# Four small moves in an attention and mixture-of-experts kernel: two in the opening, two where the experts take over

## The chip, the cores and the metric

The kernel runs on one NeuronCore of one Trainium2 chip. The core has five engines with a queue each: PE (matrix products), ACT (ScalarE), DVE (VectorE), POOL (GpSimd) and SP (SyncE, which here issues the DMAs). An engine works its queue off in order and waits on semaphores for the others. The metric is the device time of one execution in microseconds (us), the median of several runs. Times inside an execution are counted from the first instruction.

## The reference

Three stages in a row, all in float32:

```python
# 1 attention, 4 batches x 8 heads x 576 positions x 64
scores = scale * q @ k.T ; cum = cumsum(max(s, 0))
scores = where(causal, -1e9, scores + min(-(cum_i - cum_j), 0))
x = softmax(scores) @ v                      # -> 2304 tokens x 512
# 2 mixture of 8 experts, each token goes to its best one
xn, en = x / |x|, emb / |emb|
p = softmax(xn @ en.T / tau) ; e = argmax(p)
x = p[e] * (relu(x @ w1[e]) @ w2[e])         # 512 -> 1024 -> 512
# 3 gated layer
out = ((x @ wa) * (x @ wb)) @ wo             # 512 -> 1536 -> 512
```

## The kernel before

**Attention (0 to about 258 us).** Work goes by units, a unit being two heads of one batch; there are 16. For a unit, PE transposes k and q, ACT and DVE split them into a high and a low part (tiles `KH` and `sp`, `KS` and `ql`), and SP copies the queries' high part into `QS` (line 535). The scores then come from PE, DVE takes the row minimum (line 647), ACT the exponential (line 653), PE transposes the result and multiplies by v. What each engine does when is decided at build time by a small planner: the class `Sched` keeps a free time per engine and a heap of pending steps, each pushed with a ready time, an engine and a duration (`V.push(ready, engine, duration, fn)`). PE's items are taken from several lists, the first that is ready by these estimates. So a number in a push moves instructions in the engines' queues, and nothing moves at run time.

Two pushes matter here. `signs(1)` (line 1228) writes a sign pattern into eight rows of `ql`, the second of two buffers, for the second unit on. `norm` (line 1252) scales the embeddings of the experts by their norm and by tau: four DVE steps (lines 1245 to 1248) on tile `x`, which PE transposes later in `e_item`.

**Handover (258 to 300 us).** Tokens have been sorted to their experts: POOL scatters the rows into `xs` in DRAM. The experts are then taken in order of their size, not of their index. A value is loaded into all engines (line 1760), and a branch around a rarely used overflow part follows (line 1704): each engine jumps over it. Around it stand matmuls of no use, which only keep PE going (`idle`, counts in `WARM`). Then the first expert begins: `xload(0)` loads its rows `xg` from `xs` (line 1372, three DMAs), `xtr0` transposes them (line 1382) in two passes, 256 and 96 rows, four transposed slices `d` each, and ACT and DVE split them into `xh` and `xl`. `zfill(1)` writes zeros (`zrow`, line 1257) behind the second expert's rows in `xs`; since it writes the tensor that `xload(1)` reads, that load waits for it.

**Experts.** Weights come in eight blocks for each expert, of 512 KB: 0 to 3 from w1, 4 to 7 from w2. `wload2` issues the next block's DMA into tile `st` (line 243), `wsplit2` splits the oldest one that is loaded: ACT casts both halves (line 273), DVE or POOL subtract (line 281). Tiles `w0` to `w7` take the blocks of the first, third, ... expert, `v0` to `v7` those of the second, fourth, ... . Blocks 0 to 6 of the first expert are loaded and partly split in the attention stage.

In `products(e, f, prev)` PE does the first layer of slice f (line 1553, into `h`) and then the second layer of the slice before (line 1578, into `y`), which needs `hh` (ACT's relu, line 1561) and `hl` (DVE, line 1562) of that slice. Twelve matmuls make each. The loop behind it issues row loads, the next expert's transposes (`xtr`, line 1397, at slices 3 to 6) and one split and one load at a slice.

**Gated layer (about 490 us to the end).** The same with two first layers; it is not touched.

Of the kernel before, what the change touches and what calls it, by code (L numbers as in the profile page):

```python
# [34 lines left out]
PEND = (10, 1, 1)  # L35
WARM = (30, 84, 2, 0, 20, 10, 3)
LAT = 140.0
GATE = 3000.0
DRAIN = 93.0
LATP = 215.0  # L40
# [104 lines left out]
def moe_kernel(tc, q, k, v, s, emb, tau, w1, w2, wa, wb, wo, out, dbg=None):  # L145
# [36 lines left out]
    with left, right:  # L182
# [56 lines left out]

        def slot_load(src):  # L240
            t = slot([128, 1024], F32, "st")
            d = t if len(src.shape) == 2 else t.rearrange("p (a c) -> p a c", a=src.shape[1])
            nc.sync.dma_start(out=d, in_=src)
            return t
# [44 lines left out]
        if True:  # L289
# [32 lines left out]
            def ptnext():  # L322
                return pts[-TB]
# [503 lines left out]
            def e_item():  # L827
                def need():
                    return [ptnext()] if sdone[0] >= 8 else None

                def emit(end):
                    pt = ps_t.tile([128, 512], F32, name="pt")
                    for p in range(NP):
                        nc.tensor.transpose(
                            out=pt[:, E * p:E * p + E], in_=en[:, 128 * p:128 * p + 128], identity=ident[:E, :E]
                        )
                    rel = Tok()
                    pts.append(rel)

                    def f(_):  # L840
                        for h in range(2):
                            r = slice(64 * h, 64 * h + 64)
                            nc.vector.tensor_copy(
                                out=enbd[r, :, h, :], in_=pt[r, :E * NP].rearrange("p (a e) -> p a e", a=NP)
                            )

                    V.push(end, "D", 200, f, lambda t: setattr(rel, "t", t))

                return (need, 430.0, emit)
# [372 lines left out]
            def boot2():  # L1222

                blank(nc.gpsimd, kbs[1], S)
                blank(nc.gpsimd, qls[1], S - 64)
                for x in (qbs[1], z0s[1]):
                    nc.gpsimd.memset(x, 0.0)
                V.push(now[0] + 7000, "D", 840, lambda _: signs(1))
                nc.gpsimd.affine_select(
                    out=ltri, in_=ones, pattern=[[1, 128]], compare_op=ALU.is_gt, fill=0.0, base=0, channel_multiplier=-1  # L1230
                )
                nc.gpsimd.iota(iota8, pattern=[[1, E]], base=0, channel_multiplier=0, allow_small_or_imprecise_dtypes=True)
                for x in (oh, lg, sc[:, 0, :], rk, enbd, ixs):
                    nc.gpsimd.memset(x, 0.0)
                nc.gpsimd.memset(ss, 1.0)
                nc.gpsimd.memset(zrow, 0.0)
                nc.gpsimd.tensor_scalar(out=tie, in0=iota8, scalar1=-1.0, scalar2=float(E - 1), op0=ALU.mult, op1=ALU.add)
                nc.gpsimd.memset(tie[:, 0:1], FIRST + E - 1)
                for x, w in enumerate(CAPS):
                    nc.gpsimd.memset(caps[:, x:x + 1], float(w))  # L1240

            def norm():

# [7 lines left out]

                V.push(now[0] + 9000, "D", 900, f2)

# [87 lines left out]
            hp = pool(right, "hp", 2, side="right")  # L1341
            mxp = pool(right, "mxp", 4, side="right")
            keep = pool(right, "keep", 1, side="right")
# [33 lines left out]
            def xtr0():  # L1377
                t = xhs[0] = [xhp.tile([128, 4, GT], F32R, name=x)[:, :, :CAPS[0]] for x in ("xh", "xl")]
                for a0, a1 in ((0, 256), (256, CAPS[0])):
                    for d in range(4):  # L1380
                        for a in range(a0, a1, 128):
                            nc.tensor.transpose(
                                out=yb[d][:, a:a + 128], in_=xgs[0][:, a // 128, 128 * d:128 * d + 128], identity=ident
                            )
                        nc.scalar.copy(out=t[0][:, d, a0:a1], in_=yb[d][:, a0:a1])
                        nc.vector.tensor_tensor(
                            out=t[1][:, d, a0:a1], in0=yb[d][:, a0:a1], in1=t[0][:, d, a0:a1].bitcast(F32), op=ALU.subtract
                        )

            def xtr(e, d):  # L1390
# [31 lines left out]

            def wload2():
                if loaded[0] < len(jobs):
                    key = jobs[loaded[0]][0]
                    stg[key] = slot_load(slot_src(who(key[0]), key[1]))
                    loaded[0] += 1
# [329 lines left out]

            wload2()
            idle(WARM[2])
# [6 lines left out]
            count(0)  # L1766
            for j in range(4, 7):
                for x in range(2):
                    lo_op("DG"[j == 6], wstate[j], slots[0, j], 512 * x, 512 * x + 512)
            for _ in range(2):  # L1770
                misc.pop(0)()
            zfill(1)
            for _ in range(3):
                wload2()
            xtr0()
            prev = None
            for e in range(E):
                for f in range(8):
# [3 lines left out]
                    prev = (e, f)  # L1782
                    if (e, f) == (0, 1):
                        xload(1)
# [11 lines left out]
                    if e == E - 1 and f == 7:  # L1796
                        yload(1)
                    for _ in range(2 if (e, f) == (0, 1) else 1):
                        wsplit2()
                        wload2()  # L1800
# [81 lines left out]
```

## Time and profile before

| | |
|---|---|
| runs (3), median, lowest to highest | 956.17 us, 954.9 to 956.58 |
| profiled execution: time / span | 953.78 us / 952.1 us |
| PE busy | 917.8 us, 96% of the span |
| DVE, ACT, POOL busy | 516.9, 432.0, 256.4 us |
| granted TensorE clock, mean | 0.994 of full |
| PE's share of the chain that ended last | 68% |

The profile shows one execution. PE is close to full, so time is lost or gained only where PE waits; an idle engine elsewhere costs nothing by itself. "idle before <- releaser" in a row is the time an engine stood still ahead of an instruction, and the instruction that ended it. SPq is SP's queue: the time there is that of issuing a DMA, not of its transfer. [...]

### The profile page before, as it was taken

Reading aid. Unit: us, or ns where it says so; the run is one execution under the profiler, and the core shown is the slowest. Engines: PE = TensorE matmul, PEld = TensorE weight load, DVE = VectorE, ACT = ScalarE, POOL = GpSimd, SP = SyncE. Lnnn points to the kernel's source line nnn. Section 1 sums busy time; section 2 is a strip of 40 time slices with the busy share of each in tenths; the row PEclk is TensorE's granted clock in tenths of the full one; section 3 lists DMA queues with packets and bytes.
Section 4 is the critical chain, followed back from the end, with each engine's and each line's share of the span. In section 5 each row is a group of like instructions: output and inputs, shape, how many; then the busy total and the mean of one; then the engine's idle time right before and its main releaser. Section 6 shows DMA issues by size and latency. Waiting matters only on the chain.

```text
span 952.1 us, 17669 instructions
## 1 busy us (share of the span) xinstructions
PE 917.8 (96%) x6447; PEld 839.7 (88%) x6448; DVE 516.9 (54%) x1319; ACT 432.0 (45%) x1074; POOL 256.4 (27%) x308
## 2 busy tenths in 40 slices
PE   8998999999889999999999999999999999999996
PEld 7777878777669999999998999999999999999995
DVE  8788888798756343455678888732212222222112
ACT  6677888876645444455544434421211111121111
POOL 6122323256234333344303344632001001001001
PEclk9999999999999999999999999999999999999999
DMA  5774555526277667677736444412010010000000
GB/s 136 175 154 105 143 116 123 140 71 185 96 221 241 225 193 218 215 226 241 223 106 204 129 118 131 90 26 75 1 34 34 1 34 34 1 1 34 1 1 34
DMA packets 102259, 107.90 MB, mean 113 GB/s; under 512 B 58445, under 2 KB 72733, under 8 KB 102157
## 3 DMA queue, kind: packets, MB, share of 16 engines
q1 hardware_dynamic: 98573, 97.04, 36.0%
q0 software_dynamic: 3552, 9.46, 2.8%
q8 instruction: 65, 1.06, 0.5%
q14 instruction: 37, 0.30, 0.1%
q10 hardware_dynamic: 32, 0.04, 0.0%
HBM read 77.90 MB, written 20.44 MB: 103 GB/s over the span
## 4 chain that ended last, share of the span: by engine, by line
PE 68%; DMA 2%; DVE 0%; issue 0%; SPq 0%; POOLq 0%; ACT 0%; DVEq 0%; ACTq 0%
PE h L1643 16%; PE x L1643 16%; PE y L1664 14%; PE y L1578 10%; PE h L1553 10%; DMA xg<-xs 1%; PE x L1397 1%; PE x L1664 1%; PE h L1664 1%; DMA xs<-zrow 1%; DMA yt<-mx 0%; DVE xl L1631 0%; SPq L1372 0%; POOLq L1878 0%; DVE mx L1654 0%
## 5 line engine op out<-in xcount | busy, mean ns | idle before, releaser
L1654 DVE TENSOR_TENSOR mx<-x,mx 128x384 f32<-128x384 f32 x72 | 39.9, 555 | 225.1 <-PE x L1643 225.0
L1655 ACT CAST hh<-mx 128x384 fp32r<-128x384 f32 x71 | 36.4, 512 | 159.0 <-DVE mx L1654 159.0
L1649 ACT COPY mx<-h 128x384 f32<-128x384 f32 x72 | 34.5, 479 | 150.8 <-PE h L1643 149.8
L1683 POOL DMA_INDIRECT out_dram<-mx,pmt x18 | 17.6, 979 | 292.5 <-DVE mx L1682 223.2
L653 ACT ACTIVATE z<-z,mn 128x192 f32<-128x192 f32 (+3 forms) x128 | 78.2, 611 | 37.9 <-DVE mn L647 37.2
L1643 PE MATMUL h<-xh,w 128*128 128x384 f32 x288 | 79.8, 337 | 1.3 <-ACT mx L1649 1.3
L1643 PE MATMUL h<-xh,v 128*128 128x384 f32 x288 | 79.7, 337 | 0.0
L1643 PE MATMUL x<-xh,w 128*128 128x384 f32 x288 | 78.9, 334 | 0.0
L633 PE MATMUL st<-KS,QS 128*128 128x288 f32 (+3 forms) x160 | 58.7, 374 | 9.4 <-DVE mn L647 7.4
L756 PE MATMUL pt<-ident,z 128*128 128x128 f32 x448 | 63.5, 277 | 3.3 <-ACT pT L180 1.6
L281 POOL TENSOR_TENSOR w<-st,w 128x512 fp32r<-128x512 f32 (+1 forms) x43 | 47.1, 1101 | 68.1 <-ACT w L273 57.8
L647 DVE CUSTOM_DVE_ANT_0 z<-st,maskb 128x192 f32<-128x192 f32 (+3 forms) x128 | 58.7, 477 | 9.5 <-PE st L636 7.3
L1562 DVE SCALAR_TENSOR_TENSOR hl<-h,hh 128x288 fp32r<-128x288 f32 (+6 forms) x64 | 31.2, 487 | 58.8 <-ACT hh L1561 58.8
L1656 DVE TENSOR_TENSOR hl<-mx,hh 128x384 fp32r<-128x384 f32 x71 | 39.7, 559 | 41.1 <-ACT hh L1655 41.1
L800 PE MATMUL xa<-pT,vn 128*64 128x128 f32 x896 | 60.0, 278 | 1.9 <-ACT pT L180 1.6
L281 POOL TENSOR_TENSOR v<-st,v 128x512 fp32r<-128x512 f32 x32 | 43.2, 1353 | 62.5 <-ACT v L273 48.7
L1664 PE MATMUL y<-v,hh 128*128 128x512 f32 x192 | 59.8, 392 | 0.0
L756 PEld LDWEIGHTS pt<-ident,z 128*128 128x128 f32 x448 | 49.9, 141 | 11.0 <-ACT z L653 4.3
L1553 PE MATMUL h<-xh,v 128*128 128x256 f32 (+2 forms) x256 | 59.0, 304 | 0.0
L1578 PE MATMUL y<-hh,v 128*128 128x256 f32 (+2 forms) x256 | 58.0, 300 | 0.0
L1553 PE MATMUL h<-xh,w 128*128 128x288 f32 (+3 forms) x256 | 57.8, 302 | 0.0
L800 PEld LDWEIGHTS xa<-pT,vn 128*64 128x64 f32 x896 | 47.9, 137 | 11.0 <-issue 5.6
(308 smaller groups left out, 2520.0 us busy)
## 6 DMA issues: line engine op xcount, KB each, us to landing
st<-in_moe_w_dram SPq DMA_DIRECT2D x64, 512.0 KB
QS<-sp SPq DMA_DIRECT2D x62, 128.0 KB
st<-in_moe_w_a_dram SPq DMA_DIRECT2D x12, 512.0 KB
st<-in_moe_w_b_dram SPq DMA_DIRECT2D x12, 512.0 KB
st<-in_moe_w_out_dram SPq DMA_DIRECT2D x12, 512.0 KB
xg<-yt SPq DMA_DIRECT2D x6, 768.0 KB
xg<-xs SPq DMA_DIRECT2D x7, 512.0 KB
kn<-in_k_dram SPq DMA_DIRECT2D x24, 128.0 KB
```

Source lines behind the costliest of these rows:

```text
L281: e.tensor_tensor(out=o[:, 1, a:b], in0=t[:, a:b], in1=o[:, 0, a:b].bitcast(F32), op=ALU.subtract)
L633: nc.tensor.matmul(st[:m, :wp], lhsT=qs[:, h, s0 - 64:s0 - 64 + m], rhs=ks[:, h, c0:c0 + wp], start=True, stop=False)
L647: nc.vector.tensor_tensor_reduce(out=z[:m, h, c0:c0 + w], in0=st[:m, :w], in1=maskb[:m, S - kk + c0:S - kk + c0 + w], op0=ALU.add, op1=ALU ...
L653: nc.scalar.activation(out=z[:m, h, :kk], in_=z[:m, h, :kk], func=AF.Exp, scale=-1.0, bias=m1, accum_out=rsum[:m, tid(b, c), 2 * p + h:2 * ...
L756: nc.tensor.transpose(out=pt[:, 128 * x:128 * x + 128], in_=zs[i][:, h, a0:a0 + 128] if c else z0s[u % 2], identity=ident)
L800: nc.tensor.matmul(xa[64 * h:64 * h + 64, :m], lhsT=v_[:m, 2 * p + h, :], rhs=locs[i][bk, h], start=bk == 0, stop=bk == c,)
L1553: nc.tensor.matmul(ph[:, :n], lhsT=w[:, hl, 128 * f:128 * f + 128], rhs=mv[:, d, :n], start=k_ == 0, stop=k_ == 11,)
L1578: nc.tensor.matmul(ys[e][d][:, :n], lhsT=w[:, hl, c0 + 128 * d:c0 + 128 * d + 128], rhs=mv[:, :n], start=f == 0 and k_ == 0, stop=f == 7 a ...
L1643: nc.tensor.matmul(p, lhsT=w[:, hl, d, c0:c0 + 128], rhs=mv[:, d, :], start=d == 0 and k_ == 0, stop=d == 3 and k_ == 2,)
L1654: nc.vector.tensor_tensor(out=g, in0=pp[1], in1=g, op=ALU.mult)
L1656: nc.vector.tensor_tensor(out=gl, in0=g, in1=gh.bitcast(F32), op=ALU.subtract)
L1664: nc.tensor.matmul(ots[i][t], lhsT=st[:, 128 * t:128 * t + 128], rhs=w[:, hl, c0:c0 + 512], start=f == 0 and k_ == 0, stop=f == 11 and k_ ...
```

## The change

- The planner gets `signs(1)` as a step of ACT, not of DVE.
- The scaling of the embeddings is pushed 16,000 ns ahead, not 9,000 (`NORM`), and `e_item` waits for it in the plan.
- One warming matmul fewer ahead of the branch, one fewer behind it.
- The load of block 7 of the first expert, issued ahead of the branch so far, is issued behind `xtr0`, and waits on the first transposed slice of its second pass.
- The low parts of blocks 5 and 6 go to POOL (block 5 was DVE's), and three of the small steps for the gate weights come ahead of the transposes instead of two.
- `xload(1)` goes out one slice earlier, after two weight blocks were issued instead of five; the splits and loads of the first two slices are counted anew.
- A pool of 512-column tiles gets five buffers instead of four.

```diff
-WARM = (30, 84, 2, 0, 20, 10, 3)
+WARM = (30, 84, 1, 0, 20, 10, 2)
+NORM = 16000.0
...
-        def slot_load(src):
+        def slot_load(src, after=None):
             t = slot([128, 1024], F32, "st")
             d = t if len(src.shape) == 2 else t.rearrange("p (a c) -> p a c", a=src.shape[1])
-            nc.sync.dma_start(out=d, in_=src)
+            x = nc.sync.dma_start(out=d, in_=src)
+            if after:
+                tc.add_manual_dep(x.ins, after, DEP, reason="rows first")
...
-                    return [ptnext()] if sdone[0] >= 8 else None
+                    return [ptnext(), ntok] if sdone[0] >= 8 else None
...
-                V.push(now[0] + 7000, "D", 840, lambda _: signs(1))
+                V.push(now[0] + 7000, "A", 1200, lambda _: signs(1, nc.scalar.copy))
...
-                V.push(now[0] + 9000, "D", 900, f2)
+                V.push(now[0] + NORM, "D", 900, f2, lambda t: setattr(ntok, "t", t))
...
-            mxp = pool(right, "mxp", 4, side="right")
+            mxp = pool(right, "mxp", 5, side="right")
...
+                        if a0 and d == 0:
+                            first = x.ins.name
+                return first
...
-            wload2()
             idle(WARM[2])
...
-            for j in range(4, 7):
+            for x in range(2):
+                lo_op("D", wstate[4], slots[0, 4], 512 * x, 512 * x + 512)
+            for _ in range(3):
+                misc.pop(0)()
+            for j in (5, 6):
                 for x in range(2):
-                    lo_op("DG"[j == 6], wstate[j], slots[0, j], 512 * x, 512 * x + 512)
-            for _ in range(2):
-                misc.pop(0)()
+                    lo_op("G", wstate[j], slots[0, j], 512 * x, 512 * x + 512)
+            turned = xtr0()
+            wload2(turned)
             zfill(1)
-            for _ in range(3):
-                wload2()
-            xtr0()
+            wload2()
...
-                    if (e, f) == (0, 1):
+                    if (e, f) == (0, 0):
                         xload(1)
...
-                    for _ in range(2 if (e, f) == (0, 1) else 1):
-                        wsplit2()
+                    for x in range(2 if e == 0 and f < 2 else 1):
+                        if f or x == 0:
+                            wsplit2()
                         wload2()
```

SP's queue at the handover, behind the branch, before the change. `st_4885` is block 0 of the second expert, `st_4887`, `st_4889` and `st_4955` are its blocks 1 to 3; block 7 of the first expert has gone out ahead of the branch.

```order
L1372 DMA xg_4837<-xs_95 96x512
L1257 DMA xs_95<-zrow_270 736x1x256
L243 DMA st_4885<-in_moe_w1_dram 128x1024
L243 DMA st_4887<-in_moe_w1_dram 128x1024
L243 DMA st_4889<-in_moe_w1_dram 128x1024
L243 DMA st_4955<-in_moe_w1_dram 128x1024
L1374 DMA xg_5010<-xs_95 128x2x512
L1375 DMA xg_5010<-xs_95 112x512
```

The same place after the change. `st_4911` is block 7 of the first expert, `st_4914` block 0 of the second, `st_4953`, `st_4955` and `st_5015` its blocks 1 to 3.

```order
L1377 DMA xg_4834<-xs_95 96x512
L244 DMA st_4911<-in_moe_w2_dram 128x2x512
L1262 DMA xs_95<-zrow_270 736x1x256
L244 DMA st_4914<-in_moe_w1_dram 128x1024
L1379 DMA xg_4945<-xs_95 128x2x512
L1380 DMA xg_4945<-xs_95 112x512
L244 DMA st_4953<-in_moe_w1_dram 128x1024
L244 DMA st_4955<-in_moe_w1_dram 128x1024
L244 DMA st_5015<-in_moe_w1_dram 128x1024
```

Block 7 now stands between the first expert's rows and the zeros; the second expert's rows stand ahead of its block 1, not behind its block 3.

ACT's queue from the first slice on, before the change (`w7` is block 7 of the first expert, `v0` to `v3` are blocks 0 to 3 of the second, `hh` the relu of a slice).

```order
L1561 ACTIVATE hh_4946<-h0_4631 128x352
L273 CAST w7_4950<-st_4637 128x512 x2
L1561 ACTIVATE hh_5006<-h1_4632 128x352
L273 CAST v0_5013<-st_4885 128x512 x2
L273 CAST v1_5020<-st_4887 128x512 x2
L1561 ACTIVATE hh_5076<-h0_4631 128x352
L273 CAST v2_5080<-st_4889 128x512
L1488 ACTIVATE lt_4629<-lt_4629 128x160
L1561 ACTIVATE hh_5137<-h1_4632 128x352
```

And after it:

```order
L1569 ACTIVATE hh_4941<-h0_4631 128x352
L276 CAST w7_4948<-st_4911 128x512 x2
L1569 ACTIVATE hh_5006<-h1_4632 128x352
L276 CAST v0_5010<-st_4914 128x512 x2
L276 CAST v1_5017<-st_4953 128x512 x2
L1569 ACTIVATE hh_5073<-h0_4631 128x352
L276 CAST v2_5077<-st_4955 128x512
L1569 ACTIVATE hh_5137<-h1_4632 128x352
```

Casts and relus keep their order; only the exponential `lt` has left this stretch, and the casts read tiles whose loads have moved in SP's queue.

DVE's queue in the opening, before the change (`ql_191` is the second sign pattern's buffer, the four rows from line 1245 are the scaling).

```order
L1207 SCALAR_TENSOR_TENSOR xT_165<-xT_163,nb,xT_164 128x576
L1154 CAST ql_191<-pick 8x512 x2
L178 COPY pT<-pt 128x512
L395 TENSOR_TENSOR KS<-pt,KH 64x512 x2
L647 ISA z,mn<-st,maskb 128x448
L1245 TENSOR_SCALAR mn<-mn 8x1
L1246 RECIPROCAL mn<-mn 8x1
L1248 TENSOR_SCALAR x<-x,mn 8x512
L402 SCALAR_TENSOR_TENSOR ql_191<-pt,sp 64x512 x2
L395 TENSOR_TENSOR KS<-pt,KH 64x64 x2
```

And after it:

```order
L1210 SCALAR_TENSOR_TENSOR xT_165<-xT_163,nb,xT_164 128x576
L179 COPY pT<-pt 128x512
L398 TENSOR_TENSOR KS<-pt,KH 64x512 x2
L650 ISA z,mn<-st,maskb 128x448
L398 TENSOR_TENSOR KS<-pt,KH 64x64 x2
L405 SCALAR_TENSOR_TENSOR ql_191<-pt,sp 64x512 x2
L179 COPY xT_566<-xa 128x128
L1250 TENSOR_SCALAR mn<-mn 8x1
L1253 TENSOR_SCALAR x<-x,mn 8x512
L701 ISA zf_196,mn<-st,bt_529 128x64
```

The sign pattern has left DVE's queue, and the scaling stands about a dozen instructions later, ahead of the first short score pass `zf`.

## Rows read from the trace of the kernel before

**Rows 1.** PE's waits over the whole trace: engine, line, releaser: us in total, times, longest.

```profile
PE st L633 <- DVE mn L647: 7.4, 16, 1.0
PE h L174 <- PEq L1704: 2.8, 1, 2.8
PE x L1397 <- DMA xg<-xs: 1.6, 2, 1.2
```

**Rows 2.** Stretches: PE, PEld, DVE, ACT, POOL busy (instructions); PEclk; DMA; GB/s.

```profile
22.00:32.00 10.00, 8.21 (x78) 6.50 (x79) 7.72 (x29) 6.16 (x19) 0.73 (x1) 1.00 0.64 147
300.00:498.00 198.00, 198.00 (x1462) 197.82 (x1462) 97.31 (x177) 101.08 (x215) 64.35 (x49) 1.00 0.66 208
```

**Rows 3.** Timeline, PE at the handover: start, length, instruction, idle before it.

```profile
270.57 1.32 PE L1382 MATMUL y<-ident,xg 128*128 128x128 f32 x4 [0.31 <-DVE xl L1386]
278.10 0.30 PE L1578 MATMUL y<-hh,w 128*128 128x288 f32 x1
281.26 0.30 PE L1578 MATMUL y<-hh,w 128*128 128x288 f32 x1
284.27 0.41 PE L1397 MATMUL x<-ident,xg 128*128 128x128 f32 x2 [1.25 <-DMA xg<-xs]
```

**Rows 4.** Chain that ended last, 240 to 300 us: start, length, what.

```profile
266.21 3.38 DMA xg<-xs
269.80 6.20 DMA xs<-zrow
276.73 8.23 DMA xg<-xs
```

**Rows 5.** Timelines, SP's issues and POOL's first work at the handover.

```profile
244.03 0.37 SPq L243 DMA_DIRECT2D st<-in_moe_w_dram  x1
...
264.81 1.83 SPq L1372 DMA_DIRECT2D xg<-xs  x3
276.11 0.39 SPq L1374 DMA_DIRECT2D xg<-xs  x1
...
261.38 2.48 POOL L281 TENSOR_TENSOR w<-st,w 128x512 fp32r<-128x512 f32 x2 [1.75 <-POOLq L1704]
```

**Rows 6.** Timeline, ACT at the handover.

```profile
273.92 1.13 ACT L273 CAST w<-st 128x512 fp32r<-128x512 f32 x2
277.68 1.14 ACT L273 CAST v<-st 128x512 fp32r<-128x512 f32 x2 [2.07 <-DMA st<-in_moe_w_dram]
279.19 1.14 ACT L273 CAST v<-st 128x512 fp32r<-128x512 f32 x2 [0.37 <-DMA st<-in_moe_w_dram]
280.24 0.46 ACT L1561 ACTIVATE hh<-h 128x352 fp32r<-128x352 f32 x1
```

**Rows 7.** Stretches at the handover, columns as in rows 2.

```profile
261.50:264.50 3.00, 0.20 (x1) 0.00 (x0) 1.87 (x3) 1.43 (x2) 2.36 (x2) 1.00 0.05 14
264.70:268.00 3.30, 3.30 (x5) 1.22 (x5) 2.84 (x8) 0.00 (x0) 0.00 (x0) 0.50 0.55 149
283.00:284.30 1.30, 0.05 (x2) 0.06 (x1) 0.52 (x1) 0.71 (x3) 0.60 (x1) 1.00 1.05 269
...
271.10:275.00 3.90, 3.90 (x28) 3.58 (x28) 2.19 (x8) 2.22 (x7) 0.00 (x0) 1.00 0.91 186
275.00:280.60 5.60, 5.60 (x44) 5.60 (x44) 2.23 (x4) 3.07 (x8) 2.77 (x3) 1.00 1.02 377
```

**Rows 8.** Timelines of the opening: DVE, SP, PE.

```profile
18.30 1.25 DVE L1154 CAST ql<-pick 8x512 fp32r<-8x512 f32 x2
22.69 0.14 DVE L1245 TENSOR_SCALAR mn<-mn 8x1 f32<-8x1 f32 x1
23.11 0.53 DVE L1248 TENSOR_SCALAR x<-x,mn 8x512 f32<-8x512 f32 x1
...
27.18 2.48 SPq L535 DMA_DIRECT2D QS<-sp  x4
...
31.87 0.39 PE L633 MATMUL st<-KS,QS 128*128 128x256 f32 x1
```

More of the change, by code (lines that the diff above doesn't have):

```diff
@@ L1240, in boot2 @@
                     nc.gpsimd.memset(caps[:, x:x + 1], float(w))
+            ntok = Tok()
             def norm():
@@ L1381, in xtr0 @@
                         for a in range(a0, a1, 128):
-                            nc.tensor.transpose(
+                            x = nc.tensor.transpose(
                                 out=yb[d][:, a:a + 128], in_=xgs[0][:, a // 128, 128 * d:128 * d + 128], identity=ident
@@ L1421, in ringpool, with wload2 @@
                 return ringa0 if nm in ("w0", "w1", "w2", "w3") else rings[nm] if nm in rings else ringa1[0] if nm[0] == "w" else rings[nm[0]]
-            def wload2():
+            def wload2(after=None):
                 if loaded[0] < len(jobs):
                     key = jobs[loaded[0]][0]
-                    stg[key] = slot_load(slot_src(who(key[0]), key[1]))
+                    stg[key] = slot_load(slot_src(who(key[0]), key[1]), after)
                     loaded[0] += 1
```

## The prediction

> **What bounds the kernel now.** I read the list of PE's waits first: PE waits for little, and the three entries that this change touches are DVE's score passes in the attention stage (7.4 us in 16 waits), the one jump at the handover (2.8) and the rows of the second expert (1.6 in two waits) [rows 1]. Then the stretches: from 300 us on PE is busy in all of 198 us, so whatever PE loses or gains before that is kept to the end, one for one [rows 2]. So only two places matter: the opening, up to about 32 us, and the handover, 258 to 300 us. There I read PE's timeline, the chain that ended last, SP's queue and ACT's queue. In the first expert PE goes through without a gap until it reaches the transposes of rows(1), for which it waits 1.6 us in two pieces, the longer 1.25 [rows 1, 3]. The chain says why: fill(1) (zeros, 6.20 us) must have landed before rows(1) may start, and rows(1) took 8.23 us, since four weight blocks lay ahead of it in the same queue [rows 4].
>
> **The handover, step by step.** Names: (e,j) is weight block j of expert e in their order of work (the first is 0), rows(e) its token rows, fill(e) the zeros, relu(0,f) ACT's pass on slice f of the first expert.
>
> 1. Load (0,7) goes from 244.03, where the queue was empty long before anyone needed it (14 GB/s in the stretch before rows(0)), to behind the first of the four second-pass transposes: these start at 270.57 and take 1.32 us, so the first is done at 270.9 [rows 3, 5, 7]. Rows(0), issued from 264.81 to 266.64, had the queue to themselves already, so the move gives them nothing [rows 5].
> 2. SP serves in order, so fill(1) now follows (0,7): 270.9, 0.37 for the issue, 0.2 (an estimate) for SP's register steps, so 271.5 instead of 269.80 [rows 4, 5]. It needs its 6.20 us [rows 4], and its data stand behind those of (0,7), 524 KB at 377 GB/s, 1.4 us [rows 7]; (0,7) starts 0.6 us ahead, so I add 0.8. It lands at 278.5; before, at 276.0.
> 3. Rows(1) waits for that and goes out at 278.6. Rows(0) took 4.8 us from first issue (264.81) to landing (266.21 + 3.38 = 269.59) for 704 KB [rows 4, 5]; 736 KB take 5.0, so 283.6. Block (1,0) lies ahead of it and is out by then.
> 4. Load (1,1), so far ahead of rows(1), now stands behind it. Blocks in a row land 1.5 us apart (277.68 and 279.19, when ACT, which was waiting for them, could start) [rows 6], so (1,1) lands at 285.1 instead of 279.19.
> 5. What is queued behind this wait decides. ACT's order is relu(0,1), casts of (1,0), casts of (1,1), relu(0,2), as before. Relu(0,2) ran at 280.24, right after those casts, and PE wanted it at 281.26: one microsecond of slack [rows 3, 6]. Now: 285.1, 1.14 for the casts, 0.46 for relu(0,2), 0.3 (an estimate) until DVE's low part follows: PE goes on at 287.0, 5.7 us after 281.26. Rows(1) is there by then, so the old wait of 1.6 is gone [rows 1]. Net 5.7 - 1.6 = +4.1 us.
>
> Bounds of that term: the shortest time from issue to landing in that chain is 3.38 us [rows 4]; (1,1), issued at 279.4, then lands at 282.8 and the wait is 3.4, net +1.8. If fill(1) too needs only 4.8, as rows(0) did, another 1.4 goes: net +0.4. If nothing of (0,7) is hidden, 0.6 comes on top: +4.7. I take +4.1, by the rows of the very same transfers.
>
> The casts of (0,7) themselves: by the 3.38 us it lands at 274.3, ACT's casts of 1.13 us, which ran at 273.92 without a wait, end at 275.4 and relu(0,1) at 275.9 [rows 4, 6]. PE wants that at 278.10 [rows 3], so this wait is hidden; without that cover it would cost what it is late. [...]
>
> [...] One such stretch, 3.3 us at half rate, costs 1.7; I take +1.2, with 0 and 1.8 as ends. [...]
>
> Two fewer warming matmuls: one stood ahead of the jump, and it is the jump that PE waits for there [rows 1]; the third one after it ran while rows(0) were still on their way. Nothing on the path. [...] I take +0.2, 0 to 1.7.
>
> The other moves cost nothing: POOL takes four subtractions of (0,5) and (0,6) instead of two, 1.24 us each from 261.38, done at 266.4, first wanted at 281.26 [rows 3, 5]; were they late, PE would wait that long. The exponential goes into ACT's idle time ahead of the transposes.
>
> **The opening.** DVE loses the second sign pattern (1.25 us at 18.30) and the four scaling steps (22.69 to 23.64, 0.95) [rows 8], 2.2 us in all in a stretch in which PE waits for DVE; ACT gets 1.25 ahead of its pass on the next unit's queries, and the scaling lies in DVE's gaps some 5 us later. PE is idle 1.8 of the 10 us from 22 to 32 [rows 2], so 1.8 is the most. But PE's next unit, at 31.87, needs four copies which SP issues from 27.18 to 29.66 [rows 8], and SP's order there is the same and full. By the 3.38 us from issue to landing [rows 4] the last, issued at about 29.1, cannot be there much before 31.9. So PE only arrives earlier and waits. I take -0.3; ends -1.8 and, if ACT's 1.25 is in the way, +1.2.
>
> **Sum.** +4.1 + 1.2 + 0.2 - 0.3 = +5.2 us. The profiled execution took 953.78 us (span 952.1 and 1.7 around it), so 959.0 by it. The median of the runs, 956.17, is 2.4 above; the same sum on it gives 961.4, my forecast.
>
> **Rivals.**
> - The load is only half as late. The queue overlaps transfers better than step 2 to 4 have it, (1,1) lands at about 282, and the wait is 2.6. For: both shortest rows above. Against: landings 1.5 us apart in issue order [rows 6]. +0.4 to +1.8 for that term, no clock loss, -0.3: 956.3 to 957.7. That is within 0.2%.
> - Faster: (1,1) lands in time. The place is ACT's casts ahead of relu(0,2), the point is a landing by 279.4 (281.26 less 1.14, 0.46 and 0.3). Then rows(1) early is pure gain, -1.6 [rows 1], and with the opening's -0.3 to -1.8 the time is 952.8 to 954.3. For: the wait for rows(1) is real. Against: (1,1) is issued no sooner than 279.2, behind a landing of fill(1).
> - Worse: after the long wait the clock stays down for a second stretch and the later blocks, all behind, hold ACT again in the next slices: another 1.7 and 1 to 2 us, 964 to 965.
> - That the change doesn't do what it says: the order of SP's queue shows (0,7) behind rows(0) and rows(1) ahead of (1,1), so I give it no chance of its own.
>
> **How the numbers follow.** Forecast 0.66 (own range 959.3 to 963.5), half as late 0.14 (a little of it slower), faster 0.11 (a little of it within the bound below), worse 0.09. What a measurement can tell from no change is 0.2%, 1.9 us, so 954.3 to 958.1. Slower: 0.77. Same: 0.13. Faster: 0.10. The range, 955.8 to 963.6, leaves out the faster case and the worse one.
>
> **What would show it.** In the profile of the changed kernel: a wait of PE of 5 to 6 us at the first expert's second-layer products, about 281 us, released by ACT's hh or DVE's hl; ahead of it ACT idle for 3 us or more for a weight block, right before relu(0,2); no more wait for rows(1); fill(1) issued near 271.5 and rows(1) near 278.6; then a stretch at a granted 0.50. In the opening, DVE's waits shorter and PE's first product of the second unit still near 31.5. I am wrong if ACT's casts of the second block start by 280, or if PE has no wait over 2 us between 270 and 300.

## The result, and the profile after

The changed kernel took 961.17 us (median of 7 runs, 959.25 to 964.23), the kernel before 955.68 beside it (7 runs, 953.97 to 956.58): a ratio of 1.0061, 95% interval 1.0048 to 1.0074, or 5.5 us more between the medians. A second measurement on another chip gave 963.26 against 956.72, 1.0072 (1.0053 to 1.0091). The profiled execution took 960.33 us, its span 958.6, 6.5 more than before.

PE's waits answer to [rows 1] (total, times, longest):

```profile
PE st L636 <- DVE mn L650: 6.5, 15, 1.0
PE h L175 <- PEq L1712: 4.8, 1, 4.8
PE y L1586 <- ACT hh L1569: 4.5, 1, 4.5
```

The wait for the second expert's rows is gone from the list. In its place stands one of 4.5 us for `hh`, on the second-layer products of the first expert. PE's timeline shows where, and answers to [rows 3]:

```profile
270.39 0.98 PE L1387 MATMUL y<-ident,xg 128*128 128x128 f32 x7 [0.90 <-DMA xg<-xs]
271.70 1.47 PE L1387 MATMUL y<-ident,xg 128*128 128x128 f32 x4 [0.32 <-DVE xl L1391]
...
288.16 0.40 PE L1586 MATMUL y<-hh,w 128*128 128x288 f32 x1 [4.49 <-ACT hh L1569]
288.72 0.43 PE L1586 MATMUL y<-hl,w 128*128 128x288 f32 x1 [0.16 <-DVE hl L1570]
...
291.35 0.84 PE L1405 MATMUL x<-ident,xg 128*128 128x128 f32 x3
...
295.33 0.49 PE L1405 MATMUL x<-ident,xg 128*128 128x128 f32 x3
...
305.81 0.32 PE L1561 MATMUL h<-xh,v 128*128 128x352 f32 x1
```

PE's products stop at 283.67 (288.16 less the 4.49 of its wait); the transposes of rows(1), 291.35, wait for nothing; the last row is the second expert's first product. SP's queue, against [rows 5]:

```profile
264.74 3.02 SPq L1377 DMA_DIRECT2D xg<-xs  x3
272.07 0.40 SPq L244 DMA_DIRECT2D st<-in_moe_w_dram  x1
272.90 0.66 SPq L1262 DMA_DIRECT2D xs<-zrow  x1
273.77 0.46 SPq L244 DMA_DIRECT2D st<-in_moe_w_dram  x1
279.86 0.39 SPq L1379 DMA_DIRECT2D xg<-xs  x1
280.47 0.33 SPq L1380 DMA_DIRECT2D xg<-xs  x1
281.00 8.51 SPq L244 DMA_DIRECT2D st<-in_moe_w_dram  x6
```

And ACT's, against [rows 6]:

```profile
275.81 0.47 ACT L1569 ACTIVATE hh<-h 128x352 fp32r<-128x352 f32 x1 [2.37 <-PE h L1561]
276.18 1.13 ACT L276 CAST w<-st 128x512 fp32r<-128x512 f32 x2
277.40 0.47 ACT L1569 ACTIVATE hh<-h 128x352 fp32r<-128x352 f32 x1
281.31 1.14 ACT L276 CAST v<-st 128x512 fp32r<-128x512 f32 x2 [3.45 <-DMA st<-in_moe_w_dram]
286.61 1.14 ACT L276 CAST v<-st 128x512 fp32r<-128x512 f32 x2 [4.16 <-DMA st<-in_moe_w_dram]
287.65 0.46 ACT L1569 ACTIVATE hh<-h 128x352 fp32r<-128x352 f32 x1
```

After relu(0,1) at 277.40 ACT stands idle 3.45 us for block (1,0), casts it, stands idle 4.16 us for block (1,1), casts that, and only then does relu(0,2) at 287.65, whose input had been there since about 280.5 (the first-layer products of slice 2 end there). The chain that ended last says the same, against [rows 4]:

```profile
265.17 5.18 DMA xg<-xs
...
272.07 0.40 SPq L244
...
272.90 6.82 DMA xs<-zrow
...
281.00 5.59 DMA st<-in_moe_w_dram
...
287.75 0.37 ACT hh L1569
...
288.14 0.54 DVE hl L1570
...
288.72 2.83 PE y L1586 x11
```

It runs rows(0), issue of (0,7), fill(1) 6.82 us, the two issues of rows(1), block (1,1) 5.59 us, its cast, relu(0,2), low part, PE. The transfer of rows(1), 8.23 us of the old chain, has left it. Three stretches, columns as in [rows 2] (PEclk, the granted clock as a share of full, is the third number from the end):

```profile
22.00:32.00 10.00, 8.31 (x74) 7.00 (x73) 7.14 (x24) 5.05 (x16) 0.72 (x1) 0.83 0.61 142
272.00:274.00 2.00, 2.00 (x9) 1.68 (x9) 1.58 (x6) 0.97 (x5) 0.00 (x0) 0.50 0.37 91
...
288.20:292.20 4.00, 3.84 (x16) 3.61 (x17) 3.25 (x7) 1.50 (x3) 2.22 (x2) 0.59 0.95 341
```

The granted clock was 0.83 from 22 to 32 us (1.00 in [rows 2]), 0.50 in the first slice's products up to 274 (1.00 in [rows 7], 271.1 to 275), and 0.59 behind the stall.

| | before | after | difference |
|---|---|---|---|
| first matmul behind the search | 258.25 | 258.31 | +0.06 |
| rows(0) landed | 269.59 | 270.35 | +0.8 |
| first slice's `hh` | 273.56 | 275.81 | +2.25 |
| second expert's first product | 298.85 | 305.81 | +7.0 |
| end of the span | 952.1 | 958.6 | +6.5 |

All of the loss lies between 265 and 306 us. Of it 0.5 comes back later, net; among the differences there, a wait of 1.3 us of the kernel before (line 1643, for `mx`) is gone. Whether the fifth buffer did that was not tried.

### The profile page after: what moved, and what is told of

It is laid out like the page before. It is cut to its first block, busy times and chain, and to the rows that moved or that the text cites. A ratio compares the mean times of both kernels' runs of the same rounds, so it can differ in the third digit from the quotient of the medians.

```text
span 958.6 us, 17649 instructions
## 1 busy us (share of the span) xinstructions
PE 920.1 (96%) x6443; PEld 842.8 (88%) x6444; DVE 516.2 (54%) x1316; ACT 432.8 (45%) x1075; POOL 259.6 (27%) x310
## 4 chain that ended last, share of the span: by engine, by line
PE 68%; DMA 2%; DVE 1%; issue 0%; ACT 0%; SPq 0%; POOLq 0%; ACTq 0%; DVEq 0%
PE h L1651 16%; PE x L1651 15%; PE y L1672 14%; PE y L1586 11%; PE h L1561 10%; PE x L1405 1%; PE x L1672 1%; PE h L1672 1%; DMA xs<-zrow 1%; DMA st<-in_moe_w_dram 1%; DMA xg<-xs 1%; DVE xl L1639 0%; POOLq L1888 0%; DVE cv L269 0%; DVE mx L179 0%
## 5 line engine op out<-in xcount | busy, mean ns | idle before, releaser
L284 POOL TENSOR_TENSOR w<-st,w 128x512 fp32r<-128x512 f32 (+1 forms) x45 | 50.5, 1130 | 67.2 <-ACT w L276 53.3
L1586 PE MATMUL y<-hh,w 128*128 128x288 f32 (+3 forms) x256 | 57.7, 301 | 4.5 <-ACT hh L1569 4.5
```

What stands on the lines that cost most here:

```text
L284: e.tensor_tensor(out=o[:, 1, a:b], in0=t[:, a:b], in1=o[:, 0, a:b].bitcast(F32), op=ALU.subtract)
L1586: nc.tensor.matmul(ys[e][d][:, :n], lhsT=w[:, hl, c0 + 128 * d:c0 + 128 * d + 128], rhs=mv[:, :n], start=f == 0 and k_ == 0, stop=f == 7 a ...
```

## The experiments

Three theories. **Q**: queue order; relu(0,2) stands behind a cast whose block leaves late, since (0,7) and rows(1) now stand ahead of it in SP's queue. **C**: the clock, from the two warming matmuls left out. **O**: the opening. Each ratio is to the kernel before on the same chip. The chips differ: before took 970.8 us on that of the first four runs, 955.1 on that of the next four, 971.7 on that of the three behind them, so only ratios are compared between groups. On the two long ones the traces have waits that [rows 1] lacks, between 630 and 642 us, in all 4.7 us in one kernel and up to 7.6 in another; their cause stayed open. So a ratio from these two chips can hold some us that are not the handover's, and the handover is read from the traces too (the table at the end of this section).

**The changed kernel with the casts later.** Only the place of the splits changes: ACT's casts of (1,1) and its followers, and the subtractions behind them, come one to two slices later.

```diff
-                        if f or x == 0:
+                        if x < ((1, 1, 0, 1, 2, 2, 1, 1)[f] if e == 0 else 1):
                             wsplit2()
                         wload2()
+                    if e == 0 and f in (4, 5):
+                        wsplit2()
```

> The changed kernel, with one thing moved: ACT's casts of block (1,1) and the blocks behind it stand one to two slices later (none at slice 2, two each at slices 4 and 5), so that no relu stands behind a load that is still on its way. DMAs, row order and warming matmuls stay as changed. Theory Q (queue: relu(0,2) stands behind the casts of (1,1), which wait for a load behind rows(1)): PE's wait of 4.5 us at the second-layer products goes, and with it the stretch at half clock behind it, 1.7: 961.2 - 6.2 = 955.0, from 954.5 to 957 (a wait of up to 1 us may be left at the transposes). Theory C (clock: PE runs at half rate at the handover, because warming matmuls are gone): nothing here touches those, so 959 or more. Theory O (the opening made it slower): 961.

971.38 us, ratio 1.0008 (0.9988 to 1.0028), where the changed kernel had 1.0061 and 1.0072 on two other chips: the loss is no longer to be seen. PE's wait for `hh` in that trace:

```profile
PE y L1586 <- ACT hh L1569: 0.2, 1, 0.2
```

4.5 us for `hh` have become 0.2, with SP's queue, the opening, the warming, the subtractions on POOL and the fifth buffer all as changed. This is the strongest of the runs for Q.

**The changed kernel with (0,7) early again.**

```diff
+            wload2()
             idle(WARM[2])
...
-            turned = xtr0()
-            wload2(turned)
+            xtr0()
```

> The changed kernel, with block (0,7) loaded ahead of the branch again, as before the change; rows(1) stays ahead of (1,1). Theory Q: fill(1) goes out about 1.7 to 2.5 us earlier and is not pushed, (1,1) lands 2.5 us earlier than in the changed kernel (286.6), at about 284, and PE's wait falls from 4.6 to about 2; too short for a fall of the clock: 961.2 - 2.6 to - 4.3 = 957 to 958.6. Theories C and O: 961, unchanged.

973.51 us, 1.0022 (0.9999 to 1.0045): by the ratio about 2.1 us over before, roughly a third of the loss, in a wide interval. PE's wait for `hh` was 2.6 us, and behind it the granted clock was 0.50 from 296 to 298, which Q had not expected of so short a wait:

```profile
PE y L1586 <- ACT hh L1569: 2.6, 1, 2.6
```

**The kernel before with rows(1) ahead of (1,1)**, and **the kernel before with only (0,7) late**: each half of the handover's reordering alone.

```diff
-            for _ in range(3):
-                wload2()
+            wload2()
...
-                    if (e, f) == (0, 1):
+                    if (e, f) == (0, 0):
                         xload(1)
```

> The kernel before, with rows(1) alone moved ahead of block (1,1), with the loads and casts of the first two slices counted as in the changed kernel. Theory Q: fill(1) as before (landed at 276.0), rows(1) lands at 281.1, (1,1) at 282.6 instead of 279.2, relu(0,2) at 284.2: a wait of PE of about 3 where there was none, and the wait of 1.6 for rows(1) gone: +1.6, with a fall of the clock +3.3. Time of before (955.7) + 1 to + 3.3 = 956.7 to 959. Theories C and O: faster by the 1.6 of the wait that goes, 954.1.

973.9 us, 1.0031 (1.0016 to 1.0046), about +3.0: rows(1) early, which would be a gain if nothing stood behind the block that they pass, is a loss. Its profile shows the wait for `hh`, and none for rows(1):

```profile
PE y L1578 <- ACT hh L1561: 1.8, 1, 1.8
```

Net of the old 1.6 that is 0.2 us. The profiled execution was the fastest of the twelve (970.61), and where the rest of the +3.0 lies its trace does not show.

```diff
-            wload2()
             idle(WARM[2])
...
+            turned = xtr0()
+            wload2(turned)
```

> The kernel before, with block (0,7) alone loaded behind the first transpose of the second pass; rows(1) stays behind four blocks of the second expert. Theory Q: everything in SP's queue from fill(1) on comes 2.5 us later: (1,1) at 281.7, so relu(0,2) 2.3 late for PE; rows(1) at 287.5 instead of 284.9, so that PE waits there for another 2: in all +2.5, the shift of the queue: 955.7 + 2.5 = 958.2 (957 to 960 with the clock). Theories C and O: no change, 955.7.

975.64 us, 1.0052 (1.0036 to 1.0068), about +5.0, above what Q had for it. Its waits at the handover, with rows(1) still behind four blocks:

```profile
PE y L1583 <- ACT hh L1566: 2.9, 1, 2.9
PE x L1402 <- DMA xg<-xs: 2.1, 1, 2.1
```

So the late (0,7) pushes fill(1) and everything behind it: PE waits for `hh` (2.9) and then for rows(1) as well (2.1, against 1.6 before), and behind the two pauses the clock was at half:

```profile
296.00:300.00 4.00, 2.15 (x9) 1.78 (x10) 1.01 (x2) 2.45 (x6) 0.82 (x1) 0.50 1.04 353
```

The two halves make +3.0 and +5.0, the whole change +5.5 to +6.5: they are not added, since both act on the same relu.

**The kernel before with the opening alone**, and **with the warming alone**.

```diff
-                V.push(now[0] + 7000, "D", 840, lambda _: signs(1))
+                V.push(now[0] + 7000, "A", 1200, lambda _: signs(1, nc.scalar.copy))
...
-                V.push(now[0] + 9000, "D", 900, f2)
+                V.push(now[0] + NORM, "D", 900, f2, lambda t: setattr(ntok, "t", t))
```

> The kernel before with the opening's part of the change alone: the second sign pattern on ACT, the scaling later. Nothing at the handover is touched. Theory Q (the +5.5 us come from the handover's queues alone): no change, -0.5 to +1.0 us, and PE's first product of the second unit still near 31.9 to 32.3. Theory O (the opening is part of the loss, by a lower granted clock in it, 0.83 from 22 to 32 us in the profile of the changed kernel): +1.5 us or more, with that granted clock again under 0.9 from 22 to 32.

957.46 against 955.11 us, 1.0011 (0.9996 to 1.0025): no loss that can be told from none, and no gain; the +1.5 of O still lies within the interval, and the run with the old opening, below, decides. The granted clock from 22 to 32 was 1.00, so the 0.83 of the first profile does not come with the new opening each time. In this run the clock fell later, behind the wait of 1.5 us for rows(1) that the kernel before has too:

```profile
22.00:32.00 10.00, 7.80 (x77) 6.14 (x76) 7.70 (x27) 5.77 (x18) 0.72 (x1) 1.00 0.59 134
290.00:293.00 3.00, 3.00 (x15) 3.00 (x14) 2.90 (x7) 1.11 (x3) 1.30 (x1) 0.53 1.05 384
```

PE came to its score products 1.1 us sooner (25.14, where before had 26.22) and then waited for the copies of the queries, as the forecast had it:

```profile
25.14 0.40 PE L634 MATMUL st<-KS,QS 128*128 128x288 f32 x1 [1.00 <-DVE mn L648]
...
32.29 0.36 PE L634 MATMUL st<-KS,QS 128*128 128x256 f32 x1 [0.75 <-DMA QS<-sp]
```

```diff
-WARM = (30, 84, 2, 0, 20, 10, 3)
+WARM = (30, 84, 1, 0, 20, 10, 2)
```

> The kernel before with fewer warming matmuls alone: one instead of two ahead of the jump, two instead of three behind it. Theory Q: the handover's queues are as before, so only the clock can move: 0 to +1.7 us, +1.5 if the half clock of the first expert's first products (272 to 274 in the profile of the changed kernel) comes from the missing warming matmuls. Theory C (the clock is the larger part): +4 us or more. If the warming matmuls do nothing for the clock: 0, and the granted clock at the first products is 1.00 as before.

954.51 us, 0.9996 (0.9984 to 1.0008). C falls. The pause at the jump grew from 2.8 [rows 1] to 5.5 us, since PE came to it sooner, and the first slice's products still ran at full clock:

```profile
PE h L174 <- PEq L1704: 5.5, 1, 5.5
```

```profile
272.00:274.00 2.00, 1.91 (x13) 1.72 (x14) 1.15 (x5) 0.67 (x4) 0.00 (x0) 1.00 0.93 187
```

PE came to them 0.3 us later after the search than in the kernel before (13.7 us, not 13.4), and then waited 0.6 us for rows(1) instead of 1.6. That wait would hide a small loss ahead of it, so this run shows that leaving the matmuls out costs no time in this kernel, not that they do nothing for the clock.

**Can the old wait for rows(1) be had for nothing?** By Q the rows may go early if no relu stands behind a late block. Four versions of the kernel before try it. In the first, rows(1) go behind (1,0) and (1,1) and the third block's cast is made up in slice 4; in the second they go behind (1,0) alone, with the casts as in the first run above.

```diff
-            for _ in range(3):
-                wload2()
+            wload2()
+            wload2()
             xtr0()
+            xload(1)
+            wload2()
...
+                        if (e, f) != (0, 2):
                             wsplit2()
                         wload2()
+                    if (e, f) == (0, 4):
+                        wsplit2()
```

> The kernel before with the second expert's rows issued behind two of its blocks instead of four, and ACT's casts of the third block one to two slices later. Theory Q: rows(1) land about 2.5 us earlier, so PE's wait of 1.6 for them goes, and no pass of ACT's hh stands behind a block that lands late: -1.6 to 0 us. The rival, that any delay of a weight block costs PE as much as the rows gain: 0 to +2 us, with a wait for hh or for a block at the next slices.

957.17 us, 1.0022 (1.0010 to 1.0034).

> The kernel before with the second expert's rows issued behind its first block, and ACT's casts of the blocks behind them one to two slices later, so that relu(0,2) stands behind no late block. Theory Q: the wait for the rows (1.6) goes and none takes its place: -1.6 to -0.5 us, and 2.5 to 4.5 us less than the same order of loads with the casts left at their places had. The rival, that the later blocks are late for the second expert whatever ACT's order: +0.5 to +3 us, with waits of PE at the second expert's first products.

958.11 us, 1.0031 (1.0019 to 1.0044). Both missed: no wait for rows or `hh`, but one for DVE's `hl` of 2.4 and 3.0 us. The wait in the second of them, and DVE ahead of it:

```profile
PE y L1578 <- DVE hl L1562: 3.0, 1, 3.0
```

```profile
292.34 1.37 DVE L281 TENSOR_TENSOR v<-st,v 128x512 fp32r<-128x512 f32 x1 [0.34 <-ACT v L273]
293.64 1.32 DVE L1498 TENSOR_TENSOR eq<-pk,iota 128x64 f32<-128x64 f32 x1
...
295.51 1.29 DVE L1504 TENSOR_TENSOR lt<-oh,base 128x160 f32<-128x160 bf16 x1
...
297.88 0.51 DVE L1562 SCALAR_TENSOR_TENSOR hl<-h,hh 128x352 fp32r<-128x352 f32 x1
```

and POOL's work beside it:

```profile
295.36 2.57 POOL L281 TENSOR_TENSOR v<-st,v 128x512 fp32r<-128x512 f32 x2
```

The cast made up brings one more subtraction (line 281, 1.37 us at 292.34) ahead of the small steps from line 1498, and `hl`, whose relu had begun at 292.73, came at 297.88. Besides, the step of line 1504 took 1.29 us where it takes 0.33 in the kernel before: it ended within 0.2 us of the first of POOL's two subtractions. The other version has the same pair, 1.30 us beside a subtraction of POOL's. The cost of a cast moved is its subtractions too, and theory Q as I had put it left them out.

So the two other versions make the missing casts up in the second expert, where DVE has room. The first is the second of those above with one cast a slice and fewer loads ahead, the other is the first of those above with only its make-up moved:

```diff
+                    for x in range(2 if (e, f) in ((0, 0), (1, 2), (1, 3)) else 1):
+                        if (e, f) != (0, 2) and (e or x == 0):
+                            wsplit2()
+                        wload2()
```

```diff
-                    if (e, f) == (0, 4):
+                    if (e, f) == (1, 2):
                         wsplit2()
```

> The kernel before with the second expert's rows issued behind its first block, ACT's casts of the blocks behind them two slices later, and no slice of the first expert with two blocks to cast (the two missing ones are made up in the second expert's slices 2 and 3, where DVE is busy 1.2 of 4.2 us). Theory Q: neither the wait for the rows (1.6) nor one for hh or hl is left: -1.6 to 0 us against before, and 3 us or more below the same loads with the casts made up in slices 4 and 5 of the first expert, where PE waited 3.0 for DVE's hl. Theory L (the loads of the later blocks are the bound, whatever ACT and DVE do): no better than that one, +2 to +4 us, with a wait of PE at the second expert's first products.

969.91 against 971.68 us, 0.9983 (0.9968 to 0.9999).

> The kernel before with the second expert's rows issued behind two of its blocks, ACT's cast of the third block one slice later, and the missing cast made up in the second expert's slice 2 instead of the first one's slice 4. Theory Q: the 2.4 us for which PE waited for DVE's hl near 300 us with the cast made up in slice 4 are gone, and so is the wait for the rows: -1.6 to 0 us. Theory L: +1 to +3 us, as with the cast made up earlier.

970.12 us, 0.9971 (0.9956 to 0.9986): faster than the kernel before by 0.3%. From 285 to 320 us PE waits for nothing in either trace; of DVE's step at line 1504 the last one has

```profile
298.47 0.33 DVE L1504 TENSOR_TENSOR lt<-oh,base 128x160 f32<-128x160 bf16 x1
```

with POOL idle beside it. The gain, 1.7 and 2.8 us, has the size of the wait for rows(1), 1.6 [rows 1], within its interval. The early and the late make-up ran on different chips, so what the make-up's place is worth is read from two ratios, not from one comparison.

**The changed kernel with the old opening**, and **the changed kernel again**.

```diff
-                V.push(now[0] + 7000, "A", 1200, lambda _: signs(1, nc.scalar.copy))
+                V.push(now[0] + 7000, "D", 840, lambda _: signs(1))
```

(and the scaling back at its place)

> The changed kernel with the opening of the kernel before (second sign pattern on DVE, scaling at its old place); the handover is that of the changed kernel. Theory Q: the loss is the handover's: +4 to +6 us against before (0.4 to 0.6%), with PE's wait of 3.5 to 6 us for hh at the first expert's second-layer products. Theory O: the opening is 1.5 us or more of the loss, so at most +3.5 us is left.

979.67 us, 1.0088 (1.0066 to 1.0110), above both theories' figures. O falls: the loss is all there without the new opening. PE's wait for `hh` was 5.6 us, and the granted clock of the opening was low here, with the old opening:

```profile
294.34 0.61 PE L1586 MATMUL y<-hh,w 128*128 128x288 f32 x1 [5.62 <-ACT hh L1569]
```

```profile
22.00:32.00 10.00, 8.20 (x58) 6.50 (x59) 7.00 (x26) 5.07 (x14) 0.72 (x1) 0.83 0.62 136
```

> The changed kernel as it is, a second time, for its own profile and its distance to the kernel before on the chip of this run. Theory Q: +4 to +6.5 us (ratio 1.004 to 1.007), with PE's wait for hh of 3.5 to 6 us at the first expert's second-layer products. If the half clock of the first slice's products (272 to 274 us in the first profile) belongs to the change, it is there again; if it is chance of one execution, those products run at full clock here. If the changed kernel with the old opening (1.0088) was further from before only because of its chip, this run on such a chip is at 1.008 or more too; if the new opening itself helps, it stays at 1.004 to 1.007 on any chip.

963.26 us, 1.0072 (1.0053 to 1.0091). Its interval and that of the run before it overlap, so whether the new opening gains a little inside the changed kernel stays open. This run was not on a chip like that one (the kernel before took 956.7 us here), so it does not tell the chip's part either. Its rows:

```profile
PE y L1586 <- ACT hh L1569: 4.2, 1, 4.2
```

```profile
22.00:32.00 10.00, 7.65 (x78) 6.18 (x78) 7.66 (x27) 5.78 (x18) 0.73 (x1) 1.00 0.58 138
275.50:279.00 3.50, 3.50 (x15) 3.50 (x16) 0.70 (x4) 0.62 (x3) 0.00 (x0) 0.51 0.81 248
291.00:295.00 4.00, 3.93 (x16) 3.64 (x16) 3.56 (x7) 1.41 (x4) 2.62 (x2) 0.50 0.94 343
```

The stall is there again, so is the half clock of the first slice's products (275.5 to 279) and that behind the stall (291 to 295); the low clock of the opening is not.

**The handover in every trace.** From the first warming matmul behind the search to the second expert's first product, read from PE's timeline of each profile (one execution each), beside the ratio of the run:

| kernel | from, to | length | against before | ratio |
|---|---|---|---|---|
| before | 258.25, 298.85 | 40.6 | | |
| changed | 258.31, 305.81 | 47.5 | +6.9 | 1.0061 |
| changed, again | 261.57, 309.18 | 47.6 | +7.0 | 1.0072 |
| changed, old opening | 265.67, 312.82 | 47.2 | +6.6 | 1.0088 |
| changed, casts later | 267.69, 308.51 | 40.8 | +0.2 | 1.0008 |
| changed, (0,7) early | 266.19, 310.89 | 44.7 | +4.1 | 1.0022 |
| before, rows(1) ahead of (1,1) | 267.08, 309.57 | 42.5 | +1.9 | 1.0031 |
| before, (0,7) late | 266.43, 313.94 | 47.5 | +6.9 | 1.0052 |
| before, new opening | 261.99, 304.17 | 42.2 | +1.6 | 1.0011 |
| before, less warming | 258.81, 298.74 | 39.9 | -0.7 | 0.9996 |
| rows(1) behind two blocks, cast made up early | 262.54, 307.46 | 44.9 | +4.3 | 1.0022 |
| rows(1) behind one block, casts made up early | 261.56, 305.06 | 43.5 | +2.9 | 1.0031 |
| rows(1) behind one block, made up late | 267.00, 306.46 | 39.5 | -1.1 | 0.9983 |
| rows(1) behind two blocks, made up late | 265.52, 304.92 | 39.4 | -1.2 | 0.9971 |

The late (0,7) alone makes the handover as long as the whole change does, and later casts alone bring it back. The two columns agree in sign but not to the microsecond: a profile is one execution (that of rows(1) behind two blocks with the early make-up was the slowest of its twelve), and the chips' other waits are in the ratio only. With the old opening the ratio has some 2 us more than the handover; their place the trace does not show.

## Why the prediction was right, step by step

The time forecast was 961.4, the difference +5.2; measured were 961.17 and +5.5, and +6.5 on a second chip. The sign, the place and the mechanism are those of the runs: with the casts of (1,1) out of the way of relu(0,2) the loss is gone. The terms, one by one:

- **The queue (steps 1 to 5).** (0,7) went out at 272.07 (270.9), fill(1) at 272.90 (271.5), rows(1) at 279.86 (278.6), (1,1) was there at 286.6 (285.1), PE went on at 288.16 (287.0): each step 1.1 to 1.5 us behind the forecast, so the first was off and the ones between were right. The first was late because rows(0) landed 0.8 later, and PE took 0.4 longer from there to the first transposed slice of the second pass. Most of that belongs to this execution: from the first matmul behind the search to the issue of (0,7) it took 13.8 us, and 12.4 to 13.2 in the three other traces of the changed kernel with (0,7) late; the forecast has 12.65.
- **The wait.** The forecast counts it from where PE came to these products before the change, 281.26, to where it goes on: 5.7, net of the old 1.6 +4.1. Counted so it was 6.9 (288.16) and +5.3; in the second execution of the changed kernel +4.9, with the old opening +4.1. The 4.49 of the row is shorter only because PE itself came there 2.4 us later (283.7). Its lower bounds (+0.4, +1.8) were not reached in any of the three.
- **The casts of (0,7)** ended at 277.3 with relu(0,1) at 277.40, and PE, which wants that at 280.36, did not wait: hidden, as said.
- **The clock behind the stall.** +1.2 forecast, an estimate from a stretch of 3.3 us at a granted 0.50 in the kernel before [rows 7]. The second-layer products up to the transposes took 3.19 us at 288.16, at a granted 0.62, against 1.76 at 1.00 before (281.26 to 283.02, where the wait for rows(1) begins), 0.16 of it a wait, and the following slice 3.98 at 0.87 against 3.50: +1.75, and +2.4 in the second execution. The upper end, 1.8, would have been the better value.
- **The warming matmuls.** +0.2 forecast, an estimate; no run shows such a term: the warming alone was at 0.9996 (0.9984 to 1.0008), its first slice's products at a granted 1.00. In the trace the first two passes of first-layer products took 4.37 us, 3.25 before, part of them at a granted 0.50. It would be easy to book this as their price, but by the chain that ended last it costs nothing: that goes from the transposes to (0,7) and through SP's queue, and what PE loses in these products it does not wait for relu(0,2) later. With the old opening the same passes ran at 1.00; PE then waited 5.6 us instead of 4.5, and the handover took 47.2 us, not 47.5. Nor does the low clock follow the matmuls: of the six profiles with fewer of them three had 1.00 in these passes (the others 0.64, 0.72 and 0.88), of the eight with all of them four (the others 0.65 and three times 0.91). What decides it stayed open.
- **The opening.** -0.3 forecast, +0.06 in the trace by 258 us, 1.0011 (0.9996 to 1.0025) by itself. In the run of the opening alone PE arrives earlier and waits, as said. In the changed kernel's trace the low clock took the lead back: 28 products from 26.34 took 3.26 us where they took 1.75 before, and PE came to the second unit at 32.27, without a wait, against 31.87 [rows 8].
- **The other moves.** POOL's four subtractions ended at 267.39, not 266.4, and a small step of DVE's beside them took 1.26 us, where it took 0.16 before. PE waited for neither, so this cost nothing, as said:

```profile
266.17 1.26 DVE L1487 TENSOR_SCALAR nr<-nr 128x20 f32<-128x20 f32 x1
```

So the sum was too small where it counts. At the handover it has 5.5 (4.1, 1.2 and 0.2); the trace has 7.0 there, 5.3 for the wait and 1.75 for the clock, and the other two traces of this handover have 7.0 and 6.6. Then 0.5 came back later, which no term foresaw, and the median of the kernel before was 955.68 in the seven runs, not the 956.17 that the forecast stands on. That the time was met within 0.3 us is in part luck; the mechanism and the size of its terms, each within 1.2 us, are not.

Issuing (0,7) late cost 0.5% by itself (1.0052), not through its own casts, for which PE never waited, but through the queue behind it; with it early again the changed kernel was at 1.0022 (on another chip) instead of 1.0061. And as the first run shows, with every load as late as in the change but the casts' waits further back, the loss was gone too (1.0008).

The rival "half as late" would have had (1,1) land at about 282; it landed at 286.6. The rival "faster" was wrong in the same place, but its idea was not: with no relu behind a late block, rows(1) early is a gain, as the versions with steady casts show.

## What to carry to other kernels

When a load is moved past another in a queue, look not at who needs the moved one but at the instruction that waits for the one pushed back, and at what stands behind it on its engine: here a relu for the next product stood behind a cast whose result nobody needed for nearly 20 us yet. Loads may be late if their consumer stands late in its queue too (here 1.0008 instead of 1.0061); move both, and count everything the consumer brings with it (here DVE's subtraction, 1.37 us). Book a difference in one trace to an edit only when that edit alone shows it: the half clock beside the removed warming matmuls looked like their price, and the wait behind it took it up whole.

## What the runs showed of the hardware

- A DVE step with two operands (line 1504 of the kernel before) took 0.32 to 0.33 us in twelve profiles in which POOL had nothing to subtract beside it, and 1.29 and 1.30 us in the two in which one of POOL's subtractions (1.26 to 1.29 us) began just before it. The step of line 1498, with fewer elements, took 1.31 to 1.34 us in all fourteen, and in each of the seven whose rows show POOL there it stood beside such a subtraction. And a step with one operand (line 1487 of the changed kernel) took 1.23 to 1.26 us in the five profiles in which POOL had four subtractions behind the branch, 0.16 to 0.17 in the nine in which it had two and was done. Where the rows show both, the long step ended within 0.2 us of a subtraction. Why these steps are long no row shows, and no run tried any of this by itself.
- PE's pauses in the first expert and the clock behind them: the seven of 2.4 to 5.6 us were each followed by a stretch at a granted 0.50, some 3 to 7 us long (behind the pause of 2.9 a second one, 2.1, lies in it). Of three of 1.5 to 1.8 us one was followed by such a stretch (the opening alone, 0.53 from 290 to 293) and two were not (the kernel before, 1.00 from 284.3 to 290, and rows(1) ahead of (1,1), 1.00 from 292.6 to 300). Each such stretch ended while PE worked: in the changed kernel, behind the pause of 4.49, PE was busy in all of 291 to 294, and the granted clock went from 0.50 (291 to 292) by 0.82 to 1.00 (293 to 294).
- A granted clock of 0.83 from 22 to 32 us stood in two of the fourteen profiles, once with the new opening and once with the old; the others have 1.00.
